# A gated linear recurrence with an ELU layer on one core: the fourth unit's queries are turned by VectorE in 32x32 squares and moved by transfers, its keys stay with TensorE

## The chip, the cores and the metric

The kernel runs on one core of a Trainium2 chip. A core has a matmul engine (TensorE, PE in the profile), a vector engine (VectorE, DVE), a scalar engine (ScalarE, ACT), a fourth engine for odd elementwise work (GpSimd, POOL), and SyncE (SP), which only issues DMA transfers. Each engine runs its own instructions in the order in which the program has them; between engines they wait on semaphores. Data lie in HBM, in the on-chip buffer SBUF, and in PSUM, where matmuls write. The metric is the device time of one execution in microseconds (us).

## The reference

First a recurrence with a complex gate over 768 time steps, for 4 batch rows and 8 heads of width 48; then a layer of width 384 to 2048 and back, with an ELU between.

```python
# q, k, v, a_re, a_im: (4, 8, 768, 48) float32
mag = np.sqrt(a_re * a_re + a_im * a_im)
scale = np.minimum(mag, 0.999) / (mag + 1e-06)
a_re_n, a_im_n = (a_re * scale, a_im * scale)
for t in range(S):
    ar, ai = (a_re_n[:, :, t, :, None], a_im_n[:, :, t, :, None])
    new_re = ar * S_re - ai * S_im
    new_im = ar * S_im + ai * S_re
    kv = np.einsum('bhd,bhe->bhde', k[:, :, t], v[:, :, t])
    S_re, S_im = (new_re + kv, new_im)
    y[:, :, t] = np.einsum('bhd,bhde->bhe', q[:, :, t], S_re)
...
h = x @ w_in                      # x: y as (3072, 384); w_in: (384, 2048)
g = np.where(h > 0.0, h, alpha * (np.exp(np.minimum(h, 0.0)) - 1.0))
return (g @ w_out).astype(np.float32)
```

## The kernel before, in words

The 768 x 4 rows are cut into 12 *units* u = 0..11, each of 128 time steps by 2 batch rows (n = 0, 1) by 8 heads. "Fourth unit" is u = 3, "fifth" u = 4. For each unit the kernel first makes decays and angles of the gate (`squares`, `joined`, `logarithms`, `ratios`, `angles`, `turns`, on VectorE, ScalarE and, for sums over time, TensorE), then sine and cosine of the summed angle into a tile `cs` (`waves`, ScalarE), scales keys and queries by the decays (`scaled`), and multiplies them by `cs` into the tiles `kg` and `qg` with width 96 for each head (`gated`, L1011). Time lies on the 128 partitions there.

The recurrence needs `kg` and `qg` the other way about, width on the partitions: the tiles `kt` and `qt`, from which TensorE takes the scores (L1073, L1221) and the product of the queries with the carried state (L1151). There are two ways to get them.

- `transposed(u, key, n)`: for one batch row, 8 transposes of 128x96 on TensorE into PSUM (L1025), then two copies by ScalarE, into `kt` (L1027) or `qt` (L1029). Before, units 0 to 3 use it for both.
- `flipped(u, key, n)`, `moved` and `stayed`: VectorE transposes each 32x32 square in place (L1049), into a scratch; for the queries this scratch is the first part of the tile `kt`, which the keys fill later. Nine DMA transfers on SyncE's queue (`moved`, L1058, three for each block row b) carry the squares that lie off the diagonal to where they belong, and GpSimd copies the three on it (`stayed`, L1066). Units 4 to 11 use it for both.

After scores and states (`scores`, `scored`, `states`), `values` (L1142, and L1151 in `carried_products`) sums a unit's output in PSUM. ScalarE copies that out (L1163, L1168), and `seam` (L1272) issues six transfers that put the 48-wide heads together to the tile `x` of the layer. The layer itself is plain for the first three units: `inner(u, f)` multiplies 256 of the 2048 columns (six matmuls L1292) into a PSUM tile named `mlp`, of which there are three; `elu(u, f)` reads it with two steps on ScalarE (L1301, L1302) and one on VectorE (L1303), which ends the buffer's use; `project` multiplies back (L1317) and, with its last columns, copies out (L1325). From u = 2 on, products go by a scheme with fewer multiplications: `folded` (L1379), `product` (L1401) and `mult` (L1539) belong to it, and `summed_in` (L1487, L1489) and `combined` (L1360) make sums of the weights for it once. `mixed_rest` (L1519) makes sums of its input. `convert` makes another piece of weights ready (L50, L673), `warm(n)` gives TensorE n filler matmuls (L1634), `load_a`, `load_qk`, `load_v` and `fetch` issue loads.

What sets the order: each such step puts its instructions at the ends of the queues of its engines. Up to u = 3's states the order of the steps is written out by hand, in the list `first`. All later steps get a place from `put(at, fn, ...)`, 16 places to a unit, moved by a number from the table `SHIFT` where it has one; they are sorted by place. So a step that moves in the list moves on each of its engines.

```python
        nc.vector.transpose(
            out=x["flipped", key][:, :, ts(n, H)],
            in_=gates[key][:, ts(n, H * F)].rearrange("p (h b j) -> p b h j", b=F // BL, j=BL),
        )
...
        for a in range(C // BL):
            if a != b:
                nc.sync.dma_start(out=block(key, a, b), in_=nat[u]["flipped", key][ts(a, BL), b])
```

Of the kernel before, what the change touches and what calls it, by code (L numbers as in the profile page):

```python
# [505 lines left out]
def kernel(  # L506
# [1123 lines left out]
    def warm(n):  # L1630
# [98 lines left out]
    def gates_of(u, *at):  # L1729
# [15 lines left out]
        (warm, 2), (warm, 1), (scaled, 0, "k", 0), (gated, 0, 0), (scaled, 0, "q", 1),  # L1745
        *2 * [(warm, 1)], (scaled, 0, "k", 1), (warm, 1), (squares, 1), (transposed, 0, "q", 0),
        (transposed, 0, "k", 0), (convert,), (gated, 0, 1), (joined, 1), (transposed, 0, "q", 1),
        *3 * [(convert,)], (load_qk, 1), (scores, 0, 0), (logarithms, 1), (states, 0, 0),
        (powers, 1), (transposed, 0, "k", 1), (lengths, 1), (convert,), (ratios, 1), (convert,),
        (slopes, 1), (warm, 2), (noted, 1), (values, 0, 0), (decays, 1), (warm, 2), (scores, 0, 1),  # L1750
        (load_v, 1), (states, 0, 1), (angles, 1), *2 * [(warm, 2)], (scaled, 1), (noted, 0),
        (values, 0, 1), (carry_on, 0), (fetch, "in", 3), (convert,), (ends, 1), (convert,),
        (table, "trig_and_small", 1), (convert,), (seam, 0), (convert,), (warm, 1), (turns, 1),
        (convert,), (waves, 1), (inner, 0, 2), (inner, 0, 0), (fetch, "in", 4), (load_a, 2),
        (fetch, "in", 5), (table, "natural_log_exp_and_others", 1), (gated, 1, 0), (convert,),
        (gated, 1, 1), (convert,), (elu, 0, 2), (convert,), (transposed, 1, "q", 0),
        (transposed, 1, "k", 0), (convert,), (transposed, 1, "q", 1), (scores, 1, 0), (convert,),
        (states, 1, 0), (inner, 0, 4), *3 * [(convert,)], (transposed, 1, "k", 1),
        *2 * [(convert,)], (warm, 4), (values, 1, 0), (scores, 1, 1), (fetch, "in", 6),
        (fetch, "in", 7), (states, 1, 1), (convert,), (elu, 0, 0), *2 * [(convert,)], (elu, 0, 4),  # L1760
        (values, 1, 1), (seam, 1), *2 * [(convert,)], (inner, 0, 8), (inner, 0, 6), (convert,),
        (elu, 0, 8), *2 * [(convert,)], (inner, 1, 6), (inner, 1, 0), (fetch, "out", 0), (convert,),
        (inner, 1, 2), (elu, 0, 6), (convert,), (inner, 1, 4), (fetch, "out", 1), (fetch, "out", 2),
        (begun, 2), (squares, 2), (fetch, "out", 3), (joined, 2), (elu, 1, 6), *2 * [(convert,)],
        (elu, 1, 0), *2 * [(convert,)], (elu, 1, 2), *2 * [(convert,)], (elu, 1, 4),
        (logarithms, 2), (inner, 1, 12), (load_a, 3), *2 * [(convert,)], (inner, 1, 8),
        (fetch, "out", 4), (inner, 0, 10), (inner, 0, 14), (elu, 1, 12), (inner, 0, 12), (convert,),
        (fetch, "out", 5), (convert,), (noted, 2), *2 * [(convert,)], (load_v, 2), (powers, 2),
        (convert,), (elu, 1, 8), (convert,), (elu, 0, 10), (convert,), (ratios, 2),
        *3 * [(convert,)], (elu, 0, 14), (inner, 1, 10), *2 * [(convert,)], (elu, 0, 12),  # L1770
        (convert,), (elu, 1, 10), *4 * [(convert,)], (load_qk, 2), (convert,), (fetch, "out", 6),
        (project, 1, 0, 0, 4), (convert,), (inner, 1, 14), (slopes, 2), *3 * [(convert,)],
        (project, 1, 1, 0, 4), (project, 0, 0, 0, 4), (angles, 2), (lengths, 2), (fetch, "out", 7),
        (project, 0, 0, 4, 8), (elu, 1, 14), (project, 0, 1, 0, 4), (convert,), (decays, 2),
        (project, 1, 0, 4, 8), (carried, 2), *2 * [(convert,)], (table, "trig_and_small", 2),
        *2 * [(convert,)], (turns, 2), (waves, 2), (convert,),
# [63 lines left out]
    for u in range(2, NU):  # L1840
        r = (u - 2) * SLOTS
        put(r + (8 if u == PAIRED else 1.5), load_a, u)
        put(r + (8 if u < PAIRED + 3 else 10), load_qk, u)
        put(r + (8 if u < PAIRED + 3 else 12), load_v, u)
        if u == 2:
            decays_of(u, 16, 16, 17, 17, 18.4, 19.5, 19.6, 22.7, 19.8, 19.8)
            gates_of(u, 20.4, 21.6, 22.1, 22.4, 22.4, 22.6)
        else:
            sq = (r + 7.2, r + 9.6) if u < PAIRED + 4 else (r + 5.08, r + 6)
            noting = r + 11  # L1850
            decays_of(u, *sq, r + 12.8, r + 13.2, r + 13.4, r + 13.5, r + 14.9, noting, r + 15.52, r + 16.6)
# [97 lines left out]
```

## Time and profile before

| | us |
|---|---|
| time, median of three runs | 620.91 (620.36 to 625.54) |
| the profiled execution's own time | 621.49 |
| its span, from the first to the last instruction | 619.8 |
| TensorE busy in it | 605.0 (98%) |
| VectorE / ScalarE / GpSimd busy | 518.6 (84%) / 416.1 (67%) / 176.2 (28%) |
| granted TensorE clock, mean | 0.997 |

The profile is one execution. A row of its timeline gives when a group of like instructions begins (us from the span's start), how long the group takes, engine, source line, operation, the tile written and the tiles read, shape and count; in brackets at the end, where there was one, the idle time before it and whom the engine waited for. "DMA to landing" is the time from a transfer's issue to its arrival. SPq, ACTq and POOLq are the queues from which the engines issue transfers. The fourth unit's queries and keys are made between 153 and 182 us, beside the third unit's layer; the end of the second unit's recurrence lies around 64 us.

### The profile page before, as it was taken

Reading aid. Unit: us, or ns where it says so; the run is one execution under the profiler, and the core shown is the slowest. Engines: PE = TensorE matmul, PEld = TensorE weight load, DVE = VectorE, ACT = ScalarE, POOL = GpSimd, SP = SyncE. Lnnn points to the kernel's source line nnn. Section 1 sums busy time; section 2 is a strip of 40 time slices with the busy share of each in tenths; the row PEclk is TensorE's granted clock in tenths of the full one; section 3 lists DMA queues with packets and bytes.
Section 4 is the critical chain, followed back from the end, with each engine's and each line's share of the span. In section 5 each row is a group of like instructions: output and inputs, shape, how many; then the busy total and the mean of one; then the engine's idle time right before and its main releaser. Section 6 shows DMA issues by size and latency. Waiting matters only on the chain.

```text
span 619.8 us, 16981 instructions
## 1 busy us (share of the span) xinstructions
PE 605.0 (98%) x6980; PEld 549.8 (89%) x6980; DVE 518.6 (84%) x797; ACT 416.1 (67%) x681; POOL 176.2 (28%) x240
## 2 busy tenths in 40 slices
PE   8799999999999999999999999999999999999996
PEld 6678886567899999999999999998999999999996
DVE  6899999877688999888898899898899887984482
ACT  5975573776778667776777777776776777661350
POOL 2000000103114434524524434524534422422000
PEclk9989999999999999999999999999999999999999
DMA  9979739730743153745646646547673647242101
GB/s 164 180 148 133 157 110 222 155 65 21 104 77 66 47 97 84 139 96 123 126 96 123 121 99 122 127 96 121 126 130 88 140 83 131 74 88 66 53 1 33
DMA packets 192179, 65.54 MB, mean 106 GB/s; under 512 B 168116, under 2 KB 181596, under 8 KB 192092
## 3 DMA queue, kind: packets, MB, share of 16 engines
q1 hardware_dynamic: 187920, 62.72, 51.9%
q0 software_dynamic: 3520, 1.20, 1.8%
q8 instruction: 57, 0.93, 0.7%
q10 hardware_dynamic: 652, 0.44, 0.3%
q14 instruction: 30, 0.25, 0.2%
HBM read 48.91 MB, written 4.80 MB: 87 GB/s over the span
## 4 chain that ended last, share of the span: by engine, by line
PE 84%; SPq 7%; DMA 4%; DVE 3%; issue 1%; ACT 1%; POOL 0%; DVEq 0%; ACTq 0%; POOLq 0%
PE mlp L1401 27%; PE mlp L1539 14%; PE mlp L1292 10%; PE y L1539 7%; PE w L1106 4%; PE y L1317 3%; PE mlp L1317 3%; PE y L1221 3%; PE y L1151 3%; SPq L611 2%; PE w L845 2%; SPq L662 2%; PE y L1142 2%; PE w L1025 2%; SPq L1058 1%; SPq L607 1%
## 5 line engine op out<-in xcount | busy, mean ns | idle before, releaser
L1401 PE MATMUL mlp<-w_out,g 128*128 128x192 f32 x640 | 111.9, 328 | 0.0
L1401 PEld LDWEIGHTS mlp<-w_out,g 128*128 128x128 f32 x640 | 104.3, 190 | 3.3 <-DVE ee L1415 0.6
L1123 POOL TENSOR_TENSOR S<-S,T 128x384 f32<-128x384 f32 x36 | 38.0, 1057 | 149.4 <-DVE S L1121 82.7
L1379 DVE TENSOR_TENSOR g<-g 128x512 f32<-128x512 f32 x80 | 60.7, 774 | 6.3 <-PE mlp L1401 4.7
L1292 PE MATMUL mlp<-x,w_in 128*128 128x256 f32 x288 | 64.1, 381 | 0.0
L1292 PEld LDWEIGHTS mlp<-x,w_in 128*128 128x128 f32 x288 | 54.6, 191 | 8.6 <-issue 0.6
L1560 ACT ACTIVATE ee<-g 128x512 f32<-128x512 f32 x63 | 39.6, 629 | 30.1 <-DVE g L1555 27.4
L1539 PE MATMUL mlp<-x,w_in 128*128 128x128 f32 x424 | 56.3, 276 | 0.5 <-ACT g L1552 0.4
L1401 PE MATMUL mlp<-w,g 128*128 128x192 f32 x320 | 54.5, 329 | 0.0
L1539 PEld LDWEIGHTS mlp<-x,w_in 128*128 128x128 f32 x424 | 51.6, 192 | 1.0 <-ACT g L1552 0.6
L1401 PEld LDWEIGHTS mlp<-w,g 128*128 128x128 f32 x320 | 51.8, 190 | 0.6
L1272 POOL DMA_DIRECT2D x<-y x62 | 30.3, 495 | 72.5 <-ACT y L1168 40.1
L1561 ACT ACTIVATE ee<-ee 128x512 f32<-128x512 f32 x72 | 45.4, 631 | 2.3
L1564 DVE SCALAR_TENSOR_TENSOR g<-ee,g 128x512 f32<-128x512 f32 x63 | 42.4, 682 | 2.3 <-ACT ee L1561 2.3
L1552 ACT COPY g<-mlp 128x512 f32<-128x512 f32 x36 | 21.0, 585 | 29.6 <-PE mlp L1539 29.5
L1555 DVE TENSOR_TENSOR g<-g,mlp 128x512 f32<-128x512 f32 x45 | 30.8, 684 | 7.3 <-ACT g L1552 2.9
L1282 ACT ACT_TABLE_LOAD x24 | 30.8, 1283 | 0.5
L912 ACT ACTIVATE n<-w 64x384 f32<-64x384 f32 (+1 forms) x60 | 28.1, 486 | 3.8 <-PE w L897 3.0
L1539 PE MATMUL mlp<-x,g 128*128 128x128 f32 x224 | 30.0, 277 | 0.1
L1066 POOL COPY qt<-kt 32x512 f32<-32x512 f32 x24 | 24.4, 1017 | 16.7 <-PE mlp L1539 10.3
L1259 ACT COPY x<-y 128x384 f32<-128x384 f32 x20 | 8.6, 482 | 30.3 <-PE y L1151 30.3
L1539 PE MATMUL y<-x,w_in 128*128 128x128 f32 x216 | 28.5, 275 | 0.0
(219 smaller groups left out, 1384.4 us busy)
## 6 DMA issues: line engine op xcount, KB each, us to landing
w<-in_moe_w_out_dram SPq DMA_DIRECT2D x8, 768.0 KB, 4.2
g<-in_moe_w_in_dram SPq DMA_DIRECT2D x24, 256.0 KB, 3.2
g<-in_moe_w_out_dram SPq DMA_DIRECT2D x24, 256.0 KB, 2.8
w<-in_moe_w_in_dram SPq DMA_DIRECT2D x16, 288.0 KB, 6.3
vn<-in_v_dram SPq DMA_DIRECT2D x24, 192.0 KB, 4.0
qt<-kt SPq DMA_DIRECT2D x72, 64.0 KB, 2.0
kt<-cs SPq DMA_DIRECT2D x72, 64.0 KB, 2.3
q<-in_q_dram SPq DMA_DIRECT2D x11, 384.0 KB, 6.2
```

The source lines that it names most:

```text
L1123: eng.tensor_tensor(out=new_s, in0=new_s, in1=wide, op=ALU.mult)
L1272: eng.dma_start(out=x["x"][ds(j * HP + D, G), i], in_=x["y"][ds(j * HP + i * G, G)])
L1282: nc.scalar.preload_act_table_set(name)
L1292: nc.tensor.matmul(t[:, e], lhsT=w_in[:, i, ts(f + e, C)], rhs=x["x"][:, i], start=(i == 0), stop=(i == NI - 1),)
L1317: nc.tensor.matmul(x["o", n], lhsT=x["g", f // 8][:, f % 8, ts(n, C)], rhs=w_out[:, f], start=(f == 0), stop=(f == NF - 1),)
L1379: nc.vector.tensor_tensor(out=S_of(u, k, h), in0=a, in1=b, op=op)
L1401: nc.tensor.matmul(to, lhsT=a[:, m], rhs=b[:, m], start=(first and h == 0 and m == 0), stop=False, skip_group_check=True,)
L1539: nc.tensor.matmul(x["c" + c][:, ts(m, C)], lhsT=a[:, m], rhs=x["mix"][p], start=(p == BANKS[c][0] and m == 0), stop=False, skip_group_che ...
L1555: nc.vector.tensor_tensor(out=part(u, to), in0=part(u, a), in1=part(u, b), op=op)
L1560: nc.scalar.activation(out=e, in_=part(u, of), func=AF.Relu, scale=-1.0)
L1561: nc.scalar.activation(out=e, in_=e, func=AF.Exp, scale=-1.0)
L1564: nc.vector.scalar_tensor_tensor(out=part(u, to), in0=nat[u]["e", to], scalar=-1.0, in1=part(u, of), op0=ALU.add, op1=ALU.max,)
```

## The change

The queries of u = 3 leave `transposed` and take `flipped`, `moved` and `stayed`, with `gated` of the queries now ahead of that of the keys. The keys of u = 3 stay with `transposed`, whose copies fill the tile `kt` that is now the queries' scratch before. In the list `first`, `waves` of u = 3 stand ahead of `elu(2, 2)`, and `inner(0, 8)` ahead of the second half of `values` of u = 1; some `elu`, `logarithms`, `noted`, `summed_in`, `convert`, `joined` and load steps change places too. Two numbers of `SHIFT` change: the input sums of u = 4 (`mixed_rest()@4`) and one weight sum (`summed_in(18,)`) come a little later.

```diff
@@ -1666,7 +1666,7 @@
...
-        "mixed_rest()@3": 0.1, "mixed_rest()@4": 0.3, "mixed_rest()@6": 0.3, "moved('k', 0)": 1.4,
+        "mixed_rest()@3": 0.1, "mixed_rest()@4": 1.1, "mixed_rest()@6": 0.3, "moved('k', 0)": 1.4,
...
-        "summed_in(13,)": -0.8, "summed_in(16,)": -1.1, "summed_in(18,)": -0.3,
+        "summed_in(13,)": -0.8, "summed_in(16,)": -1.1, "summed_in(18,)": 0.9,
...
@@ -1745,35 +1745,35 @@
...
-        (fetch, "in", 7), (states, 1, 1), (convert,), (elu, 0, 0), *2 * [(convert,)], (elu, 0, 4),
-        (values, 1, 1), (seam, 1), *2 * [(convert,)], (inner, 0, 8), (inner, 0, 6), (convert,),
+        (fetch, "in", 7), (states, 1, 1), (inner, 0, 8), (convert,), (elu, 0, 0), *2 * [(convert,)],
+        (elu, 0, 4), (values, 1, 1), (seam, 1), *2 * [(convert,)], (inner, 0, 6), (convert,),
...
-        (elu, 1, 0), *2 * [(convert,)], (elu, 1, 2), *2 * [(convert,)], (elu, 1, 4),
-        (logarithms, 2), (inner, 1, 12), (load_a, 3), *2 * [(convert,)], (inner, 1, 8),
-        (fetch, "out", 4), (inner, 0, 10), (inner, 0, 14), (elu, 1, 12), (inner, 0, 12), (convert,),
-        (fetch, "out", 5), (convert,), (noted, 2), *2 * [(convert,)], (load_v, 2), (powers, 2),
+        (elu, 1, 0), *2 * [(convert,)], (elu, 1, 2), *2 * [(convert,)], (logarithms, 2),
+        (elu, 1, 4), (inner, 1, 12), (load_a, 3), *2 * [(convert,)], (inner, 1, 8),
...
@@ -1781,19 +1781,20 @@
...
-        (summed_in, 1), (combined, 2, 1), (combined, 4, 1), (combined, 1, 0), (summed_in, 4),
-        (summed_in, 2), (project, 0, 1, 12, 16), (combined, 2, 0), (turns, 3), (combined, 4, 0),
-        (inner, 2, 4), (inner, 2, 6), (load_a, 4), (ends, 3), (inner, 2, 2), (load_v, 3),
-        (inner, 2, 0), (elu, 2, 4), (scaled, 3), (elu, 2, 6), (summed_in, 3), (elu, 2, 2),
-        (waves, 3), (gated, 3, None, ("k",)), (elu, 2, 0), (gated, 3, None, ("q",)),
-        (project, 0, 0, 12, 16), (inner, 2, 10), (transposed, 3, "k", 0), (warm, 2), (begun, 4),
-        (folded, 2, 0, (3, 1)), (load_v, 4), (inner, 2, 8), (summed_in, 7), (squares, 4),
-        (elu, 2, 10), (load_qk, 4), (transposed, 3, "q", 0), (transposed, 3, "q", 1),
-        (summed_in, 5), (combined, 3, 0), (summed_in, 6), (joined, 4), (summed_in, 8), (elu, 2, 8),
-        (combined, 3, 1), (inner, 2, 12), (transposed, 3, "k", 1),
+        (summed_in, 1), (combined, 2, 1), (combined, 4, 1), (combined, 1, 0), (summed_in, 2),
+        (project, 0, 1, 12, 16), (combined, 2, 0), (turns, 3), (combined, 4, 0), (inner, 2, 4),
+        (inner, 2, 6), (load_a, 4), (ends, 3), (inner, 2, 2), (load_v, 3), (inner, 2, 0),
+        (elu, 2, 4), (scaled, 3), (summed_in, 4), (elu, 2, 6), (summed_in, 3), (waves, 3),
+        (gated, 3, None, ("q",)), (flipped, 3, "q", 0), (elu, 2, 2), (flipped, 3, "q", 1),
+        (moved, 3, "q", 0), (moved, 3, "q", 1), (moved, 3, "q", 2), (stayed, 3, "q"),
+        (gated, 3, None, ("k",)), (project, 0, 0, 12, 16), (elu, 2, 0), (inner, 2, 10), (warm, 2),
+        (transposed, 3, "k", 0), (begun, 4), (folded, 2, 0, (3, 1)), (load_v, 4), (inner, 2, 8),
+        (summed_in, 7), (squares, 4), (summed_in, 5), (load_qk, 4), (combined, 3, 0), (elu, 2, 10),
+        (summed_in, 6), (summed_in, 8), (elu, 2, 8), (combined, 3, 1), (inner, 2, 12),
+        (transposed, 3, "k", 1), (joined, 4),
...
@@ -1860,7 +1861,6 @@
             if u == PAIRED + 1:
                 for n in range(NB):
-                    put(r + 22 + 2 * n, transposed, u, "q", n)
                     put(r + 23 + 2.3 * n, transposed, u, "k", n)
...
```

TensorE around the fourth unit's transposes, before; `kg` and `qg` are the gated keys and queries, L1292 with 6 rows is one `inner`, L1634 is a filler:

```order
L1292 MATMUL mlp<-x,w_in 128x256 x24
L1317 MATMUL mlp<-w_out,g 128x384 x4
L1292 MATMUL mlp<-x,w_in 128x256 x6
L1025 MATMUL w<-ident,kg 96x128 x8
L1634 MATMUL mlp<-ident 128x128 x2
L1292 MATMUL mlp<-x,w_in 128x256 x6
L1025 MATMUL w<-ident,qg 96x128 x16
L1292 MATMUL mlp<-x,w_in 128x256 x6
L1025 MATMUL w<-ident,kg 96x128 x8
L1292 MATMUL mlp<-x,w_in 128x256 x6
```

TensorE at the same place after:

```order
L1292 MATMUL mlp<-x,w_in 128x256 x24
L1317 MATMUL mlp<-w_out,g 128x384 x4
L1292 MATMUL mlp<-x,w_in 128x256 x6
L1634 MATMUL mlp<-ident 128x128 x2
L1025 MATMUL w<-ident,kg 96x128 x8
L1292 MATMUL mlp<-x,w_in 128x256 x12
L1025 MATMUL w<-ident,kg 96x128 x8
L1292 MATMUL mlp<-x,w_in 128x256 x6
```

The 16 transposes of `qg` are gone, and the two fillers stand ahead of the first half of the keys.

VectorE at the same stage, before, behind the scaled queries; L1303 is the last step of an ELU and L1487 a weight sum:

```order
L1303 SCALAR_TENSOR_TENSOR g<-ee,mlp 128x512
L1487 TENSOR_TENSOR g<-g,w_in 128x512
L1303 SCALAR_TENSOR_TENSOR g<-ee,mlp 128x512
L1011 TENSOR_TENSOR kg<-k,cs 128x1536
L1303 SCALAR_TENSOR_TENSOR g<-ee,mlp 128x512
L1011 TENSOR_TENSOR qg<-q,cs 128x1536
L1379 TENSOR_TENSOR g<-g 128x512
```

VectorE there after, `kt` under L1049 being the scratch:

```order
L1303 SCALAR_TENSOR_TENSOR g<-ee,mlp 128x512
L1487 TENSOR_TENSOR g<-g,w_in 128x512
L1011 TENSOR_TENSOR qg<-q,cs 128x1536
L1049 STREAM_TRANSPOSE kt<-qg 128x3x256
L1303 SCALAR_TENSOR_TENSOR g<-ee,mlp 128x512
L1049 STREAM_TRANSPOSE kt<-qg 128x3x256
L1011 TENSOR_TENSOR kg<-k,cs 128x1536
L1303 SCALAR_TENSOR_TENSOR g<-ee,mlp 128x512
L1379 TENSOR_TENSOR g<-g 128x512
```

Gated queries and both turns come ahead of the gated keys, with one ELU step between the turns and the other behind the keys; one weight sum (L1489) has come down from further ahead.

ScalarE at the same stage, before; L981 to L985 are `waves`, L1301 and L1302 an ELU, and L1027 the first key copies:

```order
L1301 ACTIVATE ee<-mlp 128x512
L1302 ACTIVATE ee<-ee 128x512
L981 ACT_TABLE_LOAD
L981 ACTIVATE cs<-n 128x16x48
L984 ACTIVATE cs<-n 128x16x48
L985 ACTIVATE cs<-cs,quarter 128x16x48
L1301 ACTIVATE ee<-mlp 128x512
L1302 ACT_TABLE_LOAD
L1302 ACTIVATE ee<-ee 128x512
L1325 COPY o<-mlp 128x192 x2
L1027 COPY kt<-w 96x512 x2
```

ScalarE there after:

```order
L981 ACT_TABLE_LOAD
L981 ACTIVATE cs<-n 128x16x48
L984 ACTIVATE cs<-n 128x16x48
L985 ACTIVATE cs<-cs,quarter 128x16x48
L1301 ACTIVATE ee<-mlp 128x512
L1302 ACT_TABLE_LOAD
L1302 ACTIVATE ee<-ee 128x512
L1325 COPY o<-mlp 128x192 x2
L1301 ACTIVATE ee<-mlp 128x512
L1302 ACTIVATE ee<-ee 128x512
L1027 COPY kt<-w 96x512 x2
```

One ELU now comes behind `waves` and one behind the output copies L1325, ahead of the key copies.

TensorE where the second unit's recurrence ends, before; L1106 are its states, L1142 and L1151 the second half of its `values`:

```order
L1106 MATMUL w<-vn_73,kg 64x48 x32
L1142 MATMUL y_876<-a,vn_73 64x64 x2
L1142 MATMUL y_877<-a,vn_73 64x64 x2
L1142 MATMUL y_876<-a,vn_73 64x64 x2
L1142 MATMUL y_877<-a,vn_73 64x64 x2
L1142 MATMUL y_876<-a,vn_73 64x64 x2
L1142 MATMUL y_877<-a,vn_73 64x64 x2
L1142 MATMUL y_876<-a,vn_73 64x64 x2
L1142 MATMUL y_877<-a,vn_73 64x64 x2
L1151 MATMUL y_877<-qt,S 48x64 x8
L1292 MATMUL mlp<-x,w_in 128x256 x72
```

TensorE there after:

```order
L1106 MATMUL w<-vn_73,kg 64x48 x32
L1292 MATMUL mlp<-x,w_in 128x256 x6
L1142 MATMUL y_884<-a,vn_73 64x64 x2
L1142 MATMUL y_885<-a,vn_73 64x64 x2
L1142 MATMUL y_884<-a,vn_73 64x64 x2
L1142 MATMUL y_885<-a,vn_73 64x64 x2
L1142 MATMUL y_884<-a,vn_73 64x64 x2
L1142 MATMUL y_885<-a,vn_73 64x64 x2
L1142 MATMUL y_884<-a,vn_73 64x64 x2
L1142 MATMUL y_885<-a,vn_73 64x64 x2
L1151 MATMUL y_885<-qt,S 48x64 x8
L1292 MATMUL mlp<-x,w_in 128x256 x66
```

One `inner` (six matmuls) stands ahead of this half of the `values`, and 66 of the 72 behind it.

More of the change, by code (lines that the diff above doesn't have):

```diff
@@ L1747 @@
         (transposed, 0, "k", 0), (convert,), (gated, 0, 1), (joined, 1), (transposed, 0, "q", 1),
-        *3 * [(convert,)], (load_qk, 1), (scores, 0, 0), (logarithms, 1), (states, 0, 0),
-        (powers, 1), (transposed, 0, "k", 1), (lengths, 1), (convert,), (ratios, 1), (convert,),
-        (slopes, 1), (warm, 2), (noted, 1), (values, 0, 0), (decays, 1), (warm, 2), (scores, 0, 1),
+        *3 * [(convert,)], (scores, 0, 0), (logarithms, 1), (load_qk, 1), (states, 0, 0),
+        (powers, 1), (transposed, 0, "k", 1), (lengths, 1), (ratios, 1), (convert,), (slopes, 1),
+        (convert,), (warm, 2), (noted, 1), (values, 0, 0), (decays, 1), (warm, 2), (scores, 0, 1),
         (load_v, 1), (states, 0, 1), (angles, 1), *2 * [(warm, 2)], (scaled, 1), (noted, 0),
@@ L1754 @@
         (convert,), (waves, 1), (inner, 0, 2), (inner, 0, 0), (fetch, "in", 4), (load_a, 2),
-        (fetch, "in", 5), (table, "natural_log_exp_and_others", 1), (gated, 1, 0), (convert,),
+        (table, "natural_log_exp_and_others", 1), (gated, 1, 0), (convert,), (fetch, "in", 5),
         (gated, 1, 1), (convert,), (elu, 0, 2), (convert,), (transposed, 1, "q", 0),
@@ L1764 @@
         (begun, 2), (squares, 2), (fetch, "out", 3), (joined, 2), (elu, 1, 6), *2 * [(convert,)],
-        (elu, 1, 0), *2 * [(convert,)], (elu, 1, 2), *2 * [(convert,)], (elu, 1, 4),
-        (logarithms, 2), (inner, 1, 12), (load_a, 3), *2 * [(convert,)], (inner, 1, 8),
-        (fetch, "out", 4), (inner, 0, 10), (inner, 0, 14), (elu, 1, 12), (inner, 0, 12), (convert,),
-        (fetch, "out", 5), (convert,), (noted, 2), *2 * [(convert,)], (load_v, 2), (powers, 2),
+        (elu, 1, 0), *2 * [(convert,)], (elu, 1, 2), *2 * [(convert,)], (logarithms, 2),
+        (elu, 1, 4), (inner, 1, 12), (load_a, 3), *2 * [(convert,)], (inner, 1, 8),
+        (fetch, "out", 4), (inner, 0, 10), (inner, 0, 14), (inner, 0, 12), (convert,),
+        (fetch, "out", 5), (convert,), (elu, 1, 12), *2 * [(convert,)], (load_v, 2), (powers, 2),
         (convert,), (elu, 1, 8), (convert,), (elu, 0, 10), (convert,), (ratios, 2),
[L1770 to L1776, printed above, removed]
+        *3 * [(convert,)], (elu, 0, 14), (noted, 2), (inner, 1, 10), *2 * [(convert,)],
+        (elu, 0, 12), (convert,), (elu, 1, 10), *4 * [(convert,)], (load_qk, 2), (convert,),
+        (project, 1, 0, 0, 4), (convert,), (inner, 1, 14), (slopes, 2), *2 * [(convert,)],
+        (fetch, "out", 6), (convert,), (project, 1, 1, 0, 4), (project, 0, 0, 0, 4), (angles, 2),
+        (lengths, 2), (fetch, "out", 7), (project, 0, 0, 4, 8), (elu, 1, 14), (project, 0, 1, 0, 4),
+        (convert,), (decays, 2), (project, 1, 0, 4, 8), (carried, 2), *2 * [(convert,)],
+        (table, "trig_and_small", 2), *2 * [(convert,)], (turns, 2), (waves, 2), (convert,),
         (table, "natural_log_exp_and_others", 2), (scaled, 2), (project, 0, 1, 4, 8), (convert,),
@@ L1783 @@
         (convert,), (ratios, 3), (convert,), (lengths, 3), (project, 1, 0, 12, 16), (slopes, 3),
-        (convert,), (transposed, 2, "q", 0), (project, 1, 1, 12, 16), (angles, 3), (scored, 2),
+        (transposed, 2, "q", 0), (project, 1, 1, 12, 16), (convert,), (angles, 3), (scored, 2),
         (opened,), (states, 2, 0), (valued, 2), *3 * [(convert,)], (seam, 2),
         (project, 0, 0, 8, 12), (combined, 1, 1), (summed_in, 0), (noted, 3), (carried, 3),
-        (summed_in, 1), (combined, 2, 1), (combined, 4, 1), (combined, 1, 0), (summed_in, 4),
-        (summed_in, 2), (project, 0, 1, 12, 16), (combined, 2, 0), (turns, 3), (combined, 4, 0),
-        (inner, 2, 4), (inner, 2, 6), (load_a, 4), (ends, 3), (inner, 2, 2), (load_v, 3),
-        (inner, 2, 0), (elu, 2, 4), (scaled, 3), (elu, 2, 6), (summed_in, 3), (elu, 2, 2),
-        (waves, 3), (gated, 3, None, ("k",)), (elu, 2, 0), (gated, 3, None, ("q",)),
-        (project, 0, 0, 12, 16), (inner, 2, 10), (transposed, 3, "k", 0), (warm, 2), (begun, 4),
-        (folded, 2, 0, (3, 1)), (load_v, 4), (inner, 2, 8), (summed_in, 7), (squares, 4),
-        (elu, 2, 10), (load_qk, 4), (transposed, 3, "q", 0), (transposed, 3, "q", 1),
-        (summed_in, 5), (combined, 3, 0), (summed_in, 6), (joined, 4), (summed_in, 8), (elu, 2, 8),
-        (combined, 3, 1), (inner, 2, 12), (transposed, 3, "k", 1),
+        (summed_in, 1), (combined, 2, 1), (combined, 4, 1), (combined, 1, 0), (summed_in, 2),
[9 more added lines that the diff above has]
+        (transposed, 3, "k", 1), (joined, 4),
     ]
```

## The prediction

> **What bounds the kernel now.** I read the page first: busy time, then the chain that ended last, then the stretches by clock time, and last the rows of each engine around the places that the change touches. Time is TensorE's.
>
> ```profile
> span 619.8 us, 16981 instructions
> PE 605.0 (98%) x6980; PEld 549.8 (89%) x6980; DVE 518.6 (84%) x797; ACT 416.1 (67%) x681; POOL 176.2 (28%) x240
> PE 84%; SPq 7%; DMA 4%; DVE 3%; issue 1%; ACT 1%; POOL 0%; DVEq 0%; ACTq 0%; POOLq 0%
> ```
>
> In the table by stretches the columns are the stretch, its length, TensorE's busy time (and instructions), the granted clock, the DMA share and GB/s.
>
> ```profile
> 48.00:64.00 16.00, 15.81 (x333) 1.00 0.89 136
> 64.00:76.00 12.00, 12.00 (x87) 1.00 0.65 123
> 153.00:182.00 29.00, 29.00 (x176) 1.00 0.65 96
> 182.00:553.00 371.00, 368.68 (x4757) 1.00 0.54 106
> ```
>
> TensorE has no gap at the two places where its instructions move, 64 to 76 us and 153 to 182 us. So work taken off it there is worth its full length, and a new wait there costs its full length: little later gives it back, since of the 371 us behind only 2.3 are gaps, and these follow from work that starts later. The profiled execution took 621.49 us (span 619.8 and 1.69 around it); the median of the three runs is 620.91. I sum on the profile and then move by that 0.58.
>
> **The transposes that go.** The fourth unit's queries are 16 instructions on TensorE in one block.
>
> ```profile
> 165.89 2.75 PE L1292 MATMUL mlp<-x,w_in 128*128 128x256 f32 x12
> 168.48 1.04 PE L1025 MATMUL w<-ident,kg 128*96 128x128 f32 x8
> 169.35 0.61 PE L1634 MATMUL mlp<-ident 128*128 128x128 f32 x4
> 169.80 2.76 PE L1292 MATMUL mlp<-x,w_in 128*128 128x256 f32 x12
> 172.39 1.91 PE L1025 MATMUL w<-ident,qg 128*96 128x128 f32 x16
> 174.14 2.76 PE L1292 MATMUL mlp<-x,w_in 128*128 128x256 f32 x12
> ```
>
> From the block's start to the next matmul's: 174.14 - 172.39 = **-1.75 us**. The same way one `inner` takes 168.48 - 165.89 = 2.59 us, half the key transposes 0.87, the fillers 0.45. ScalarE's four copies of these queries go too, and count for nothing: it waits for TensorE here.
>
> **ELU behind the waves.** On ScalarE, sine and cosine of the fourth unit now stand ahead of the ELU of `inner(2, 2)`.
>
> ```profile
> 158.96 0.63 ACT L1302 ACTIVATE ee<-ee 128x512 f32<-128x512 f32 x1
> 162.20 1.28 ACT L981 ACT_TABLE_LOAD   x1
> 165.10 0.94 ACT L985 ACTIVATE cs<-cs,quarter 128x768 f32<-128x768 f32 x1
> 165.94 0.58 ACT L1301 ACTIVATE ee<-mlp 128x512 f32<-128x512 f32 x1
> 167.83 0.63 ACT L1302 ACTIVATE ee<-ee 128x512 f32<-128x512 f32 x1
> 166.07 1.76 DVE L1011 TENSOR_TENSOR kg<-k,cs 128x1536 f32<-128x1536 f32 x1 [3.17 <-ACT cs L985]
> 168.49 0.69 DVE L1303 SCALAR_TENSOR_TENSOR g<-ee,mlp 128x512 f32<-128x512 f32 x1 [0.67 <-ACT ee L1302]
> 169.10 1.75 DVE L1011 TENSOR_TENSOR qg<-q,cs 128x1536 f32<-128x1536 f32 x1
> 170.77 1.41 DVE L1379 TENSOR_TENSOR g<-g 128x512 f32<-128x512 f32 x2
> 209.98 1.83 DVE L1049 STREAM_TRANSPOSE kt<-qg 128x768 f32<-128x768 f32 x2
> 211.73 1.72 DVE L1011 TENSOR_TENSOR kg<-k,cs 128x1536 f32<-128x1536 f32 x1
> ```
>
> The last two rows are the fifth unit, which is already turned on VectorE. Now the ELU before (the row at 158.96) ends at 159.59, and the table load follows at once. Cosine ended 166.04 - 162.20 = 3.84 us after the load began, so it ends at 163.43 now, 2.6 earlier. The ELU of `inner(2, 2)` begins 0.10 before that, at 163.33, and ends 168.46 - 165.94 = 2.52 later, at 165.85. VectorE: gated queries from 163.46, 1.67 to the next instruction (169.10 to 170.77); first turn from 165.13, 0.87 each ((211.73 - 209.98) / 2); the ELU's last step from 166.0, done 0.69 later at 166.69; second turn from 166.6 to 167.56; gated keys from 167.5 to 169.25.
>
> `inner(2, 10)` on TensorE needs the PSUM buffer that this last step frees. Before it began at 165.89 without a wait; now at 166.69: **+0.8 us**. That stays if VectorE or ScalarE runs as in these rows; if the ELU were done by 165.1 it would be nothing. The key transposes then come up at 166.69 + 2.59 + 0.45 = 169.73, and the gated keys are ready at 169.25: 0.48 to spare, so this added wait costs nothing.
>
> **Keys behind the transfers.** VectorE turns the queries into `kt`, from where nine transfers and three copies take them; ScalarE's copies of the transposed keys into `kt` must wait for these. That wait is new.
>
> ```profile
> 169.12 1.07 ACT L1027 COPY kt<-w 96x512 f32<-96x512 f32 x2 [0.23 <-PE w L1025]
> 172.18 0.63 ACT L1302 ACTIVATE ee<-ee 128x512 f32<-128x512 f32 x1
> 211.87 5.61 SPq L1058 DMA_DIRECT2D qt<-kt  x9
> DMA to landing us min/median/max: 3.8/3.8/3.8
> DMA to landing us min/median/max: 2.0/2.2/4.1
> ```
>
> The first landing row is the fifth unit's group at 211 to 219 us, the second all transfers of this kind (L1058) in the run. The nine are issued 0.62 apart, the first 0.06 after the second turn (211.87 against 211.81): here 167.62. The second key copy needs the fifth transfer, issued at 167.62 + 4 x 0.62 = 170.1 and landed at 172.1 (with 2.0) or 173.9 (with 3.8). Queued behind it on ScalarE: two squares of the fifth unit and the ELU of `inner(2, 10)`. From the second copy's start (169.12 + 0.55) to that ELU's end (172.81) it took 3.14 before, and VectorE adds 0.69: the buffer for `inner(2, 14)` is free at 175.9 or 177.7. TensorE wants it at 169.73 + 0.87 + 2.59 + 2.59 + 0.87 = 176.65. So **0**, or +1.05 at the slow landing; the point is a landing of 2.75 us. I take 0, by the median of 2.2.
>
> ```profile
> 201.71 1.82 POOL L990 TENSOR_TENSOR k<-k,n 128x768 f32<-128x768 f32 x1 [0.25 <-ACT n L912]
> ```
>
> On SP the nine stand ahead of two stores and the fifth unit's values, queries and keys, about 5.6 us later for those; the first to use them, the scaling of the keys at 201.7, comes some 25 us after that, so nothing. The three copies on GpSimd stand ahead of the sum of squares of the fifth unit, which is read only by ScalarE's logarithms, behind the last ELU of this stage: nothing.
>
> ```profile
> 171.74 2.11 POOL L734 TENSOR_TENSOR n<-n 128x768 f32<-128x768 f32 x1 [13.14 <-ACT n L728]
> 172.09 2.31 DVE L1487 TENSOR_TENSOR w_in<-w_in 128x512 f32<-128x512 f32 x1
> 211.94 3.30 POOL L1066 COPY qt<-kt 32x512 f32<-32x512 f32 x3 [4.16 <-DVE kt L1049]
> L1066 POOL COPY qt<-kt x3: 607/607/1967, 211.9 to 214.6; 32x512 f32<-32x512 f32 x3
> ```
>
> In these rows VectorE and GpSimd hold each other up: the 128x512 step took 2.31 us beside GpSimd's 2.11, where its like takes 0.69; and of three equal copies one took 1.97 beside the gated keys, which took their usual 1.72. The later starter waits. Here the gated keys start (167.5) before the copies may (167.6), so GpSimd waits and TensorE loses nothing. The Trainium skill's page "SBUF — State Buffer", section "SBUF: two separate sides", has it as a rule: the two share a port pair as an exclusive lock, whoever starts first keeps it for the instruction. The trace agrees, 2.31 against 2.11.
>
> **The seam of the second unit.** `inner(0, 8)` moves ahead of the second half of its `values`, so one `inner` less lies between these and `inner(1, 6)`, which reads what the seam's transfers bring.
>
> ```profile
> 63.50 0.81 PE L1142 MATMUL y<-a,vn 64*64 64x64 f32 x32
> 64.82 31.35 PE L1292 MATMUL mlp<-x,w_in 128*128 128x256 f32 x144
> L1272 ACTq DMA_DIRECT2D x<-y x3: 514/602/1602, 65.5 to 67.7; - x3
> DMA to landing us min/median/max: 2.2/2.5/2.8
> ```
>
> Count from the end of `values` (64.82 before). The last transfer is issued 2.9 later (67.7) and lands after 5.1 to 5.7. Before, two `inner` (5.18) and two of the six matmuls of the third (0.86) came first: needed at 6.04, hidden by 0.3 to 0.9. Now one `inner` comes first: needed at 3.45, so a wait of 1.6 to 2.2. If the 1602 ns issue is a usual 0.6 the time, 1.0 less: 0.6 to 1.2. The moved `inner` fills no gap in return: from 48 to 64 us TensorE is short of full by 0.2 in all. I take **+1.2**: between the two, nearer the low one, because the DMA engines had a share of 1.08 when those transfers were issued and 0.07 at the time where they are issued now.
>
> ```profile
> 64.00:66.00 2.00, 1.00 1.08 172
> 68.00:70.00 2.00, 1.00 0.07 16
> ```
>
> The other moves (ELU and logarithms of the third unit on ScalarE, one conversion on VectorE, one weight sum and one input mix later) lie where TensorE's next need is an `inner`, 2.59, away, and the steps are 0.4 to 1.9 long: 0, at most 0.3 either way.
>
> **Sum**: -1.75 + 0.8 + 0 + 1.2 = +0.25. Profile 621.7, by the median 621.2: no change that a run can show. About 1%, 6.2 us, is what a measurement of this kernel can tell from no change.
>
> **The rivals.**
> *All covered.* The new waits come out shorter than by these rows: the seam's transfers land within 3.5, the ELU is ready. For it: both margins hang on single issues of 1.6 and on 0.8 of order. Against it: the rows. -1.75 + 0.2 = 619.3. Chance 0.25.
> *Slower: key copies held by the transfers.* ScalarE stands at the key copy until the fifth transfer has landed, over 2.75 us, and the ELU behind it frees `inner(2, 14)` late: +1.05 at 3.8, with the seam at 2.2: -1.75 + 0.8 + 1.05 + 2.2 = +2.3, 623.2. For it: the first such group, the fifth unit's, read 3.8. Against: the median is 2.2. Chance 0.17. The Trainium skill's page "VectorE: DVE Perf Modes", section "Rules for kernel authors", speaks the same way: 128x128 transposes belong on TensorE where PSUM will do, VectorE's are 32x32. Here the path from turn to last block is 5.6 + 2 to 4 us against 1.75, and is hidden unless the key copy meets it.
> *Slower by the port.* The three copies get in ahead of the gated keys: 3 x 0.607 = 1.82, less the 0.48 to spare, +1.3: 622.5. Only if GpSimd starts first, which the rows speak against. Chance 0.05.
> That the change doesn't do what it says is out: the order shows 16 transposes fewer.
>
> **Numbers.** Forecast 621.2, chance 0.5; 0.03 is left for the unforeseen. The range takes the all-covered case and nearly the whole slower one, 619.0 to 623.2. Only something outside these cases moves it by 6.2: faster 0.02, same 0.95, slower 0.03.
>
> **What would show it.** Right: 16 fewer L1025 on TensorE, a gap of about 0.8 ahead of the `inner` at 166 and about 1.2 near 70, none before the key transposes, none ahead of the last `inner` by 179. All covered: no such gaps. Slower: ScalarE idle at L1027 for over 2 us, released by a transfer, and a TensorE gap near 177. It would be wrong if the waits fall elsewhere, or if the fifth unit's stage, 205 to 232, shifts by more than 0.5.

## The result, and the profile after

The changed kernel took 626.05 us (median of 18 runs, 622.86 to 630.79), the kernel before 621.47 (18 runs, 619.02 to 628.80): a ratio of 1.0084, 95% interval 1.0059 to 1.0109. That is 4.6 us slower where 0.3 was forecast, and above the range of 619.0 to 623.2. Ratios and their intervals leave out the few runs over 1.5% above the fastest of the same kernel, and they are not quotients of the medians, which count every run. The profiled execution took 624.54 us, with a span of 622.8, 3.0 more than before. First the page of the changed kernel: span, busy time, and the chain that ended last by engine.

```profile
span 622.8 us, 16967 instructions
PE 602.8 (97%) x6964; PEld 546.4 (88%) x6964; DVE 519.5 (83%) x799; ACT 414.2 (67%) x677; POOL 177.5 (29%) x243
PE 83%; DVE 5%; DMA 4%; ACT 4%; issue 2%; SPq 1%; POOL 0%; ACTq 0%; DVEq 0%; POOLq 0%
```

TensorE works 2.2 us less (602.8 against 605.0), the 16 transposes among it, and the span is longer: it waits more. Its stretches, with the columns as before the prediction:

```profile
48.00:64.00 16.00, 16.00 (x309) 1.00 0.98 148
64.00:76.00 12.00, 9.36 (x84) 1.00 0.63 120
153.00:182.00 29.00, 28.27 (x132) 1.00 0.60 99
182.00:553.00 371.00, 368.66 (x4758) 1.00 0.55 106
```

Of the two places that were full, one now has a gap of 2.64 us and the other one of 0.73; the 371 us behind have gaps of 2.3 as before. TensorE at both, after; the brackets hold the wait and who ended it:

```profile
66.58 4.03 PE L1292 MATMUL mlp<-x,w_in 128*128 128x256 f32 x16
73.26 9.09 PE L1292 MATMUL mlp<-x,w_in 128*128 128x256 f32 x41 [2.64 <-DMA x<-y]
...
166.55 2.74 PE L1317 MATMUL mlp<-w_out,g 128*128 128x384 f32 x8
170.03 2.86 PE L1292 MATMUL mlp<-x,w_in 128*128 128x256 f32 x12 [0.73 <-DVE g L1303]
173.17 1.04 PE L1025 MATMUL w<-ident,kg 128*96 128x128 f32 x8
180.10 2.76 PE L1292 MATMUL mlp<-x,w_in 128*128 128x256 f32 x12
182.69 1.46 PE L1401 MATMUL mlp<-w_out,g 128*128 128x192 f32 x8
```

The first wait is that for the second unit's seam, the second that of `inner(2, 10)` for its ELU. Where the 3.0 us came up is seen by following the same instruction through both timelines:

| start of | before | after | later by |
|---|---|---|---|
| the first `inner` (L1292) | 44.96 | 44.53 | -0.43 |
| the first `project` (L1317) | 96.01 | 98.37 | 2.36 |
| the first `project` behind the third unit's recurrence | 146.40 | 149.55 | 3.15 |
| the third unit's first `inner` | 152.95 | 156.10 | 3.15 |
| the first `product` (L1401) | 180.20 | 182.69 | 2.49 |
| the fifth unit's scores (L1221) | 228.41 | 231.15 | 2.74 |
| span | 619.8 | 622.8 | 3.0 |

Between the first two rows lies the seam, +2.8; by itself it cost 3.2, since 0.4 had been gained ahead of it. From the end of `values` to the first `project` TensorE did twelve `inner` before, in 31.19 us (64.82 to 96.01), 2.60 each. Now it does eleven, which need 28.59, and takes 31.79 (66.58 to 98.37). The bracket shows less, 2.64, because it counts from the modelled end of the last matmul and not from the place where the next one would have begun, 70.03 (one `inner` and two matmuls of the next, 3.45, behind 66.58). The fourth unit's stage gives -0.66 (27.25 to 26.59). Of the +0.79 around 140 to 149 us, 0.65 are waits in which the profile shows nothing that TensorE waited for (0.26 and 0.71, against 0.32 before); in the experiments below they were 0.43 to 0.98 with and without the change's parts, so they are not laid to it.

### The profile page after: what moved, and what is told of

It reads as the page before. It is cut to its first block, busy times and chain, and to the rows that moved or that the text cites. A ratio compares the mean times of both kernels' runs of the same rounds, so it can differ in the third digit from the quotient of the medians.

```text
span 622.8 us, 16967 instructions
## 1 busy us (share of the span) xinstructions
PE 602.8 (97%) x6964; PEld 546.4 (88%) x6964; DVE 519.5 (83%) x799; ACT 414.2 (67%) x677; POOL 177.5 (29%) x243
## 4 chain that ended last, share of the span: by engine, by line
PE 83%; DVE 5%; DMA 4%; ACT 4%; issue 2%; SPq 1%; POOL 0%; ACTq 0%; DVEq 0%; POOLq 0%
PE mlp L1401 26%; PE mlp L1539 14%; PE mlp L1292 10%; PE y L1539 7%; PE w L1106 4%; PE mlp L1317 3%; PE y L1317 3%; PE y L1221 3%; PE y L1151 3%; PE w L845 2%; PE y L1142 2%; PE w L1025 2%; DMA x<-y 1%; PE mlp L1634 1%; PE w L897 1%
## 5 line engine op out<-in xcount | busy, mean ns | idle before, releaser
L1401 PE MATMUL mlp<-w_out,g 128*128 128x192 f32 x640 | 111.9, 328 | 0.0
L1401 PEld LDWEIGHTS mlp<-w_out,g 128*128 128x128 f32 x640 | 104.3, 190 | 3.3 <-DVE ee L1415 0.6
L1292 PE MATMUL mlp<-x,w_in 128*128 128x256 f32 x288 | 64.8, 382 | 4.7 <-DMA x<-y 4.0
L1292 PEld LDWEIGHTS mlp<-x,w_in 128*128 128x128 f32 x288 | 53.7, 190 | 14.7 <-DMA x<-y 3.2
L1401 PE MATMUL mlp<-w,g 128*128 128x192 f32 x320 | 54.5, 329 | 0.0
L1401 PEld LDWEIGHTS mlp<-w,g 128*128 128x128 f32 x320 | 51.8, 190 | 0.6
L1561 ACT ACTIVATE ee<-ee 128x512 f32<-128x512 f32 x72 | 45.4, 631 | 2.3
L1066 POOL COPY qt<-kt 32x512 f32<-32x512 f32 x27 | 26.7, 989 | 24.7 <-DVE kt L1049 14.4
```

The costliest lines, as they stand in the source:

```text
L1292: nc.tensor.matmul(t[:, e], lhsT=w_in[:, i, ts(f + e, C)], rhs=x["x"][:, i], start=(i == 0), stop=(i == NI - 1),)
L1401: nc.tensor.matmul(to, lhsT=a[:, m], rhs=b[:, m], start=(first and h == 0 and m == 0), stop=False, skip_group_check=True,)
L1561: nc.scalar.activation(out=e, in_=e, func=AF.Exp, scale=-1.0)
```

## The experiments

The theory now: the loss is TensorE's wait at the seam, made by moving `inner(0, 8)`; the fourth unit's part gains a little. Rivals: the transfers of the queries cost the time; or the granted clock does. Each kernel is compared with the kernel before, run beside it. Of long lines of the list the edits show only the part around what changes.

**The inner put back.** In the changed kernel:

```diff
-        (fetch, "in", 7), (states, 1, 1), (inner, 0, 8), (convert,),
+        (fetch, "in", 7), (states, 1, 1), (convert,),
...
-        (seam, 1), *2 * [(convert,)], (inner, 0, 6),
+        (seam, 1), *2 * [(convert,)], (inner, 0, 8), (inner, 0, 6),
```

> The changed kernel with inner(0, 8) put back behind the second half of the second unit's values; all else of the change stays. Theory (the two new waits of TensorE: 2.64 us at the seam of the second unit, 0.73 us for the ELU of inner(2, 2), less the transposes): no gap on TensorE between 62 and 76 us, the 0.73 gap near 167 stays, and the span is some 2.4 to 2.9 us shorter than that of the changed kernel, 622.8 - 2.6 = 620.2; ratio to the kernel before 0.999 to 1.002. Rival (the queries' transfers and copies cost the time, in the stage from 153 us on): ratio stays at 1.006 to 1.010. Rival (a lower granted clock in more of the changed kernel's runs): the shortest runs come down by 2.6, but the longest stay near 630 as often as with the whole change.

Measured: 620.55 us (12 runs, 618.70 to 624.34), ratio 0.9989 (0.9966 to 1.0012), span 620.2. Its stretch from 64 to 76 us:

```profile
64.00:76.00 12.00, 12.00 (x98) 1.00 0.59 114
```

The ELU's wait is still in its timeline of TensorE:

```profile
167.72 2.86 PE L1292 MATMUL mlp<-x,w_in 128*128 128x256 f32 x12 [0.73 <-DVE g L1303]
```

With the `inner` back, the loss is gone and all else of the change stays. It came down by 5.5 us in the median, against a gap of 2.64 in the one profile. Its longest run took 624.34, so the runs near 630 did not stay, as they would by the rival of a lower clock.

**The inner alone.** The kernel before, with only that move:

```diff
-        (fetch, "in", 7), (states, 1, 1), (convert,), (elu, 0, 0), *2 * [(convert,)], (elu, 0, 4),
-        (values, 1, 1), (seam, 1), *2 * [(convert,)], (inner, 0, 8), (inner, 0, 6), (convert,),
+        (fetch, "in", 7), (states, 1, 1), (inner, 0, 8), (convert,), (elu, 0, 0), *2 * [(convert,)], (elu, 0, 4),
+        (values, 1, 1), (seam, 1), *2 * [(convert,)], (inner, 0, 6), (convert,),
```

> The kernel before with one thing of the change alone: inner(0, 8) stands ahead of the second half of the second unit's values. Theory: the same TensorE gap at L1292 near 70 us, 2.2 to 2.9 us, released by a seam transfer; span 2.3 to 2.9 us longer than before; ratio 1.004 to 1.005. Rival (the queries' part costs the time): no more than 0.5 us longer, ratio within 0.999 to 1.001.

Measured: 627.03 us (6 runs), ratio 1.0076 (1.0047 to 1.0105). The move alone makes the whole loss, and more than the 1.004 to 1.005 that its gap was priced at. TensorE of this run at the seam:

```profile
72.31 7.97 PE L1292 MATMUL mlp<-x,w_in 128*128 128x256 f32 x28 [2.92 <-DMA x<-y]
```

Its stretches of 2 us there, with the granted clock behind the count of instructions:

```profile
72.00:74.00 2.00, 1.69 (x6) 0.82 0.71 93
74.00:76.00 2.00, 2.00 (x6) 0.50 0.86 338
76.00:78.00 2.00, 2.00 (x9) 0.83 0.07 28
```

Right behind the gap the clock was halved for some 3.4 us. Until then this was in no sum of mine.

**The queries alone.** The kernel before, with the list from `(summed_in, 1), (combined, 2, 1)` on as in the change, and without the line that puts `transposed(u, "q", n)`:

> The kernel before with the fourth unit's part of the change alone: its queries flipped and moved, the list from the third unit's weight sums on as in the change; inner(0, 8) and the other earlier moves left as before, and the two numbers of the table too. Theory: the stage from the first inner of the third unit to the first product (27.25 us before, 26.59 in the changed kernel) is 0.6 to 0.8 us shorter than before, one gap of 0.7 us ahead of inner(2, 10), no gap near 70; ratio 0.997 to 1.001. Rival (this part costs time by its transfers and the wait of the key copies): ratio over 1.002.

Measured: 621.05 us (12 runs, 619.90 to 628.62), ratio 1.0017 (0.9982 to 1.0052), span 618.9. The stage from the third unit's first `inner` (152.22) to the first `product` (178.81) takes 26.59 us, 0.66 less than before, with a wait of 0.72 for the ELU. By its profile this part gains; by its times it makes no difference that can be told, and the rival's loss of over 0.2% isn't shut out by the interval.

**The weight loads held back.** Why did the seam's transfers land so late? In the changed kernel's timeline, ScalarE's issues of the seam's transfers and SyncE's of weight loads:

```profile
67.28 1.80 ACTq L1272 DMA_DIRECT2D x<-y  x3
68.53 1.80 SPq L662 DMA_DIRECT2D w<-in_moe_w_in_dram  x4
```

ScalarE's issues by that line, from the first start to the last, and the landings that show of all six transfers:

```profile
L1272 ACTq DMA_DIRECT2D x<-y x3: 514/600/602, 67.3 to 68.5; - x3
DMA to landing us min/median/max: 1.6/1.6/4.2
```

The median landed after 1.6 us, the latest after 4.2. The four loads (two of 288 KB, two of 96) start as the seam's last transfers, of 16 KB each, are issued. They wait for a conversion by VectorE (L50) to free their buffer. So two reasons were possible: the loads hold the transfers up, or one `inner` is too short a cover anyway. The change to tell them apart (it adds two lines, so line numbers are higher by 2):

```diff
     def fetch(kind, m):
         t, dst, pairs = weights_of(kind, m)
+        if (kind, m) == ("in", 7):
+            nc.vector.memset(t[:, 0:1], 0)
...
-        (fetch, "in", 7), (states, 1, 1), (inner, 0, 8), (convert,),
+        (states, 1, 1), (inner, 0, 8), (convert,),
...
-        (elu, 0, 8), *2 * [(convert,)], (inner, 1, 6),
+        (elu, 0, 8), (fetch, "in", 7), *2 * [(convert,)], (inner, 1, 6),
```

> The changed kernel, with the four loads of the eighth weight piece (issued at 68.5 us, beside the seam's transfers) held back until VectorE's last step of the ELU of inner(0, 8) is done: a write of two columns by VectorE into the piece's buffer, behind that step, is what they wait for. No conversion moves. Theory (these loads delay the seam's last transfers): loads issued at 71 us or later, seam transfers land within 1.6 to 2.5 us of their issue, TensorE's gap near 70 falls from 2.64 to 0 to 0.9 us, ratio 0.999 to 1.003. Rival (one inner is too short a cover by itself): gap 2.2 to 4, ratio 1.004 to 1.010.

Measured: 621.65 us (12 runs, 619.69 to 626.23), ratio 1.0004 (0.9979 to 1.0029), span 618.6. The timelines of ScalarE, SyncE and TensorE:

```profile
66.76 1.80 ACTq L1274 DMA_DIRECT2D x<-y  x3
70.64 1.75 SPq L664 DMA_DIRECT2D w<-in_moe_w_in_dram  x4
66.06 13.59 PE L1294 MATMUL mlp<-x,w_in 128*128 128x256 f32 x60
79.89 8.04 PE L1294 MATMUL mlp<-x,w_in 128*128 128x256 f32 x36 [0.23 <-DVE g L1305]
88.08 8.11 PE L1294 MATMUL mlp<-x,w_in 128*128 128x256 f32 x36 [0.15 <-DVE g L1305]
```

And the seam's landings:

```profile
DMA to landing us min/median/max: 1.6/1.6/1.6
```

Same `inner`, same conversions, loads 2.1 us later: all landings that show are at 1.6, and 60 matmuls run without a gap where 16 did. One `inner` is enough cover where the loads come later: the loss came from the moved `inner` and these loads together. Two short waits for ELUs are left; the way from `values` to the first `project` takes 29.96 us (66.06 to 96.02), 1.4 over the 28.59 of eleven `inner`. The Trainium skill's page "DMA: Bandwidth & Descriptors", section "Issuing engines are not separate DMA queues", says that transfers from different engines run on the same 16 DMA engines and interleave; the trace agrees, 4.2 beside the loads and 1.6 without.

**The conversions later.** An earlier run on the same question moved VectorE's conversions behind the ELU of `inner(0, 8)`:

```diff
-        (values, 1, 1), (seam, 1), *2 * [(convert,)], (inner, 0, 6), (convert,),
-        (elu, 0, 8), *2 * [(convert,)], (inner, 1, 6),
+        (values, 1, 1), (seam, 1), (inner, 0, 6),
+        (elu, 0, 8), *5 * [(convert,)], (inner, 1, 6),
```

> The changed kernel, with VectorE's five weight conversion steps around the seam all behind the ELU of inner(0, 8), so that the weight buffer comes free later and SyncE issues its four weight loads (L662, at 68.5 us in the changed kernel) some 3 us later, behind the seam's transfers. Theory (the seam's last transfer landed late, 4.2 us against 1.6 for the other two that show a landing, because these loads share the DMA engines with it): the transfers land within 1.6 to 2.5 us and the TensorE gap near 70 shrinks from 2.64 to 0 to 0.9 us. Rival (one inner is too little cover, whatever the loads do): gap stays at 2.2 to 2.9.

Measured: 626.07 us (9 runs), ratio 1.0058 (1.0014 to 1.0102). No wait for a transfer is left at the seam, and all landings were 1.6, as expected; but the time did not come back. Another wait came, for an ELU whose last step stands behind the late conversions on VectorE, and TensorE stood 1.86 us ahead of its last state matmul, where the profile shows nothing that it waited for:

```profile
67.11 0.20 PE L1106 MATMUL w<-vn,kg 64*64 64x48 f32 x1 [1.86 <-issue]
81.49 18.83 PE L1292 MATMUL mlp<-x,w_in 128*128 128x256 f32 x86 [1.84 <-DVE g L1303]
```

In this profile the clock was also low in the opening (0.50 from 44 to 48 us). So the ELU's wait is not shown to be the whole loss of this kernel.

**The ELU back ahead of the waves.** In the changed kernel:

```diff
-        (summed_in, 3), (waves, 3),
-        (gated, 3, None, ("q",)), (flipped, 3, "q", 0), (elu, 2, 2), (flipped, 3, "q", 1),
+        (summed_in, 3), (elu, 2, 2), (waves, 3),
+        (gated, 3, None, ("q",)), (flipped, 3, "q", 0), (flipped, 3, "q", 1),
```

> The changed kernel with elu(2, 2) back ahead of the fourth unit's waves; all else stays. Theory: the TensorE gap of 0.73 us ahead of inner(2, 10) (near 170 us) goes, that at the seam stays (2.2 to 2.9), and what the waves lose (about 1.2 us of ScalarE) comes back as a wait for the gated keys of at most 0.8 us; span 0 to 0.7 us shorter than the changed kernel's. Rival (the flips and transfers themselves hold TensorE): the gap stays or moves to the key transposes with 0.7 us or more.

Measured: 630.97 us (4 runs), ratio 1.0163 (1.0120 to 1.0206). The small wait went, and a greater one came, for the gated keys:

```profile
178.68 1.08 PE L1025 MATMUL w<-ident,kg 128*96 128x128 f32 x8 [2.21 <-DVE kg L1011]
```

That is 1.48 us worse (2.21 - 0.73), not at most 0.8; the stage from the third unit's first `inner` to the first `product` takes 28.08 us against the changed kernel's 26.59. By this profile, the place the change gives this ELU is the better one. The rest of this kernel's loss is the seam again, which nothing touched: two waits, and the clock behind them.

```profile
74.15 0.67 PE L1292 MATMUL mlp<-x,w_in 128*128 128x256 f32 x2 [2.95 <-DMA x<-y]
76.08 8.13 PE L1292 MATMUL mlp<-x,w_in 128*128 128x256 f32 x29 [1.27 <-DMA x<-y]
```

**The gap filled.** In the changed kernel, 14 matmuls that nobody reads, ahead of `inner(1, 6)`:

```diff
-        (elu, 0, 8), *2 * [(convert,)], (inner, 1, 6),
+        (elu, 0, 8), *2 * [(convert,)], (filled, 14), (inner, 1, 6),
```

> The changed kernel with 14 filler matmuls (some 3.2 us on TensorE, into a PSUM buffer that nobody reads) ahead of inner(1, 6), where TensorE waited 2.64 us for the seam's transfers. It takes the idle time away, not the time. Theory (a gap of TensorE at the seam costs more than its length, since the granted clock then falls to 0.50 for some 3 us in part of the runs, as in two of the three other profiles with that gap): no stretch at 0.50 between 66 and 84 us, and fewer runs above 626; median some 2 us under the changed kernel's, ratio 1.003 to 1.005. Rival (the clock falls for other reasons, and the gap costs its length alone): the same spread as the changed kernel, ratio 1.007 to 1.010.

Measured: 625.03 us (12 runs, 621.87 to 630.64), ratio 1.0064 (1.0029 to 1.0098). The landing was later in this profile, at 5.8 at the most, so 1.09 us of the wait were left; the clock stayed at 1.00 from 66 to 84 us. Of its 12 runs 4 took over 626 us, against 3 of 10 of the changed kernel beside it: not fewer, as the theory had it. This profile needs 33.16 us from `values` to the first `project` (66.23 to 99.39), 4.6 more than eleven `inner`: the fillers stand where the wait was. The ratio lies between the two expectations and decides nothing.

**The changed kernel again.**

> The changed kernel as it is, once more, beside the filled one on the same chip. Theory: a gap at the seam of 2.6 to 4.3 us, which varies with where the weight loads meet the seam's last transfers; ratio 1.006 to 1.010. If the gap were the same 2.64 in every profile, the spread of the times would be the clock's alone.

Measured: 625.12 us (10 runs, 623.12 to 632.65), ratio 1.0046 (1.0013 to 1.0078), a little under what was expected. Its seam, with two waits:

```profile
73.06 0.67 PE L1292 MATMUL mlp<-x,w_in 128*128 128x256 f32 x2 [2.46 <-DMA x<-y]
74.74 9.53 PE L1292 MATMUL mlp<-x,w_in 128*128 128x256 f32 x36 [1.01 <-DMA x<-y]
```

The clock behind them:

```profile
74.00:76.00 2.00, 1.26 (x3) 0.60 0.42 69
76.00:78.00 2.00, 2.00 (x6) 0.54 0.81 327
```

So the wait is no fixed size. In the four profiles with the `inner` moved, the loads beside the seam and nothing filled in, it was 2.64, 2.92, 3.47 and 4.22 us; in three of the four, all but the first, the clock was halved right behind it. In the six without a wait of over 1.1 us there (before, the inner put back, the queries alone, the loads held back, the conversions later, the gap filled) the clock stayed at 1.00 from 70 to 80 us.

No kernel here beats the one before: the two best, at 0.9989 and 1.0004, can't be told from it.

## Why the prediction was wrong

**The step that failed** is the seam's term, +1.2 with 2.2 at the most: "nearer the low one, because the DMA engines had a share of 1.08 when those transfers were issued and 0.07 at the time where they are issued now". The need was counted rightly, 3.45 behind `values`. The last issue came at the quick end of what was counted, 1.9 behind them (66.58 to 68.5). What failed is the landing. It was taken from the quiet of a stretch of the trace of before, as if what filled the next stretch would not be there. SyncE's row in the timeline of before, in that quiet, whose transfers fill what follows:

```profile
69.08 1.74 SPq L662 DMA_DIRECT2D w<-in_moe_w_in_dram  x4
```

The changed kernel's stretches there; behind the clock (1.00) stand the DMA share and GB/s:

```profile
66.00:68.00 2.00, 1.00 0.00 0
68.00:70.00 2.00, 1.00 0.31 66
70.00:72.00 2.00, 1.00 1.07 234
```

Before, the seam's last issue began at 67.7 and the loads 1.4 behind it; now both begin at 68.5. The seam's first issue had moved by 1.8 us and its last by 0.8, and the loads came 0.6 earlier. So the seam ran into them, and stood in a share of 1.07 for its last transfers. The latest landed after 4.2 us, not 2.2 to 2.8. Counted as in the prediction, from the need at 70.03 to the start at 73.26, the wait is 3.2 us in that profile, where 0.6 to 2.2 was allowed; in others it is longer. So the low end, 0.6, came from a reading that did not hold, and the high end was too low.

**A term was missing**: what a gap of TensorE does to its clock. Three of four such gaps were followed by some 3.4 us at half the clock, about 1.7 us of lost time each. From the end of `values` to the first `project` the four profiles take 31.79, 33.74 (65.37 to 99.11), 34.39 (66.98 to 101.37) and 35.24 us (67.59 to 102.83) for the eleven `inner` that need 28.59. So the seam costs 3.20, 5.15, 5.80 and 6.65 us, 5.2 on average: 1.3 of clock (three fourths of 1.7) and 3.9 of waiting. Less the stage's 0.66 that makes +4.5, beside the 4.6 (626.05 - 621.47) and 3.6 (625.12 - 621.55) of the two comparisons. The size of the clock's part rests on few profiles. The filled gap, made to test it, gave no clear answer, and runs over 626 us come up without the seam's gap too: 3 of the 29 of the kernel before beside it, and 3 of the 12 of the queries alone.

**What was right**, by its own steps. The transposes: the block's run from `inner(2, 10)` to the first `product` fell from 14.31 to 12.66 us, -1.65 for the -1.75. The ELU behind the waves: a wait of 0.73, and `inner(2, 10)` 3.48 behind the start of the `project` ahead of it instead of 2.58, +0.90 for the +0.8; the key transposes without a wait behind it, as said. Keys behind the transfers, and the port, in the timelines of the three engines:

```profile
175.53 0.58 ACT L1027 COPY kt<-w 96x512 f32<-96x512 f32 x1 [1.10 <-DMA qt<-kt]
178.77 0.69 DVE L1303 SCALAR_TENSOR_TENSOR g<-ee,mlp 128x512 f32<-128x512 f32 x1 [1.50 <-ACT ee L1302]
170.79 1.72 DVE L1011 TENSOR_TENSOR kg<-k,cs 128x1536 f32<-128x1536 f32 x1
171.00 3.65 POOL L1066 COPY qt<-kt 32x512 f32<-32x512 f32 x3 [9.24 <-DVE kt L1049]
```

The landings of the queries' transfers (L1058) from 160 to 185 us:

```profile
DMA to landing us min/median/max: 2.0/2.0/2.0
```

ScalarE did stand at the second key copy, 1.10 us, until the transfers landed, after 2.0 and so under the 2.75 from which it would count. The ELU it held up freed its buffer at 179.46, and TensorE came to it at 180.10. GpSimd's copies began 0.2 behind the start of the gated keys, which took their usual 1.72. Both slower rivals fail on these rows. The rival that all is covered had the seam wrong; the loads held back show what it would have been, 621.65 at a ratio of 1.0004, with the stage as it is and the two short waits for ELUs.

The forecast gave 0.95 to a move within 1%, and 0.84% lies within it; but it was of no change that a run can show, and this change is clear of that (1.0059 to 1.0109), outside the range. The chance of 0.03 for slower by over 1% left too little room for a wait with no upper bound from a row.

## What to carry to other kernels

A step that moves by two microseconds meets the neighbours of its new place: before a transfer is priced by a quiet stretch, look up which transfers are issued at that time and behind it, and by which other engine's step they are set free. A wait of TensorE may cost more than its length, since the clock can fall behind it. And where cover runs short, it can be better to hold back the load that is not needed yet than to put back the work that covered it.

## What was not expected of the hardware

The half clock behind a gap. In the kernel with the `inner` alone it followed a single wait of 2.92 us, and lasted from about 73.3 to 76.7 us. The Trainium skill's page "TensorE: Matmul & The Clock Gate", section "Part 1: The HAM clock gate (the "warmup" mystery)", has the clock fall to half after at least one idle window of about 3.4 us. The trace agrees in the length of the slow stretch. In the length of the gap it depends on the count. By the brackets, 2.92 us, and 2.46 and 1.01 with 0.67 of work between, were followed by it, and 2.64 once was not. Counted from the place where the next matmul would have begun, TensorE started nothing for 3.49 us in the first (65.37 + 3.45 = 68.82, to 72.31), for 3.06 and 1.25 in the second, and for 3.23 in the one with no slow clock behind it; by this count only the split gap is followed by a slow clock without a stretch of 3.4 us. Which count the clock goes by, no run here shows. The clock was also halved in the opening, where no such gap stands ahead: in the profile of before from 42 to about 45.4 us, behind waits of 0.20 and 0.37 us in the 15 us ahead. What sets that off is open.
